# Attention's result and the normalised residual of six tiles: transposed by DMA as 16-bit planes

## The chip, the cores and the metric

The kernel runs on one core of a Trainium2 chip. The metric is the time on the device in microseconds (us). TensorE is called PE in the profile (its weight loads PEld), VectorE DVE, ScalarE ACT, GpSimd POOL and SyncE SP. The kernel before takes 514.92 us, the median of three runs (514.51 to 515.2).

## The reference

One transformer block on 2,048 positions of 512 features, in float32: layer norm, attention with 32 heads of 16 features, in which each position sees itself and seven others at distances 2, 4, ... 14, the product with `wo`, the residual; then layer norm, a product with `w1` (1,792 features), relu squared, a product with `w2`, the residual.

```python
def _A_ref(x, wqkv, wo):
    qkv = (x @ wqkv) ...                       # 32 heads of 16
    off = jnp.arange(8) * 2
    idx = pos[:, None] - off[None, :]          # masked where below zero
    logits = jnp.einsum("bhsd,bhswd->bhsw", q, kg) * scale
    o = jnp.einsum("bhsw,bhswd->bhsd", _softmax(logits), vg)
    return o.reshape(B, S, D) @ wo
def _B_ref(x, w1, b1, w2, b2):
    h = jnp.einsum("bsd,df->bsf", x, w1) + b1
    r = jnp.where(h > 0, h, 0)
    return jnp.einsum("bsf,fd->bsd", r * r, w2) + b2
h = x + _A_ref(_layernorm(x), wqkv, wo)
out = h + _B_ref(_layernorm(h), w1, b1, w2, b2)
```

## The kernel before

**Tiles.** The positions are cut into 16 tiles of 128 rows (t = 0 to 15), four of which make a unit u. Every product is made in three: each float32 operand is split into a high part in the format of the fast matmul (`hi`, L140, a cast on ACT) and a low part, the rest (`lo`, L143, a subtraction). `mm3` (L216) multiplies high by high, low by high and high by low, 4 matmuls each over the four blocks of 128 features.

**Transposes.** A product needs its left operand with features on the partitions. `transposes` (L196) turns the four 128x128 blocks of a tile by four matmuls with an identity into a PSUM bank. `o_T` (L562) turns attention's result o of a tile and has ACT take the high part (`hi_T`) and DVE the low part (`lo_T`) from the bank. `h_T` (L610) does so with the normalised residual `hn`, into the tiles `hh` and `hl` that the product with `w1` reads. For the last unit (tiles 12 to 15) `last_h_T` (L632) and `split_last` (L645) also form sums and differences of blocks, for a scheme with fewer products.

**Order of the work.** It is written out by hand; each engine runs its instructions in the order of the program. The program is cut into slots. `at(d, ...)` puts a chore into the list of the slot d later, `after` into a second list. `end_slot` (L112) issues the first list, then as much of attention as fits (`pump`, L409), then the second list. Attention (`attention`, L267) is a stream of steps on DVE with a cost for each; `pump` takes steps until DVE's planned time reaches PE's, the costs being multiplied by `SLOW` (1.01 in the first phase, then 1.12, then 1.08). POOL adds up the weighted values (`add_up`, L398). `pump(until=s)` first issues what is left of attention for tiles 2s and 2s+1.

**Phases.** First the product with `wqkv`, its results stored to DRAM in chains from which attention loads windows of keys and values. In the later part of this phase (`first_phase`, L918) tiles 0 to 3 go through attention's tail, `wo` and the norm. Then the loop at L997 makes three passes u = 0, 1, 2, each of 17 slots. In slot p, PE runs `mlp1` (L790: the product with `w1` for one block of 128 hidden features, 12 matmuls; p < 14) and `mlp2` (L797: that with `w2` for the block three slots earlier, 12 matmuls; p > 2). Beside them run the next unit's tiles t = 4(u+1) + i: `load_h` (slots LH), `o_T` (slots OP = 6, 7, 12, 13), `wo_product` (L596, slots WP = 8, 9, 13, 14; it stands ahead of `mlp1` in its slot), and `h_T` in slots 15 and 16 (14 and 15 in pass 2). After that comes a last stage for tiles 12 to 15.

`wo_product` issues its 12 matmuls and orders four chores: `h_add` (L575; DVE adds the residual and takes the statistics with `norm_stats`, L148: a statistics and an aggregate instruction; POOL then makes the reciprocal root), `h_norm` (L581; ACT applies the norm into `hn`), `add_b2` (POOL) and `spill` (to DRAM). `act_stats` (L169) is another way to the statistics, used for some tiles of x: ACT sums the row, then the squares of the differences from the mean.

**What is shared.** In the loop `mm0` and `mm1` are the only PSUM banks for `mlp1`, `wo` and the transposes, taken in turn; ACT's relu (`hidden`, L781) frees that of `mlp1` in the next slot. Rows of 128 x 512 come from one pool of 15 buffers (`row`, L96). All loads and stores but a few go through SP's queue, in order: windows (L243, L256), weights (L959), stashed low parts of `w2` (L989, L994), x (L560), the residual (L590, L594). A DMA that must wait holds those behind it.

Of the kernel before, what the change touches and what calls it, by code (L numbers as in the profile page):

```python
# [7 lines left out]

F32 = mybir.dt.float32
F32R = mybir.dt.float32r  # L10
AF = mybir.ActivationFunctionType
ALU = mybir.AluOpType
X = mybir.AxisListType.X
# [2 lines left out]
P = 128  # L16
KB = D // P
FB = F // P
R = 4
RI = 2  # L20
# [7 lines left out]
NEG = -4.0e9  # L28
ROWS = 15
LAG = 3  # L30
SLOW = 1.01, 1.12, 1.08
DELAY = 3
WJ = 2
XT = (9, 11), (7, 8)
OT = 4, 5, 10, 12
WO = 7, 9, 13, 15
HT = 20, 20, 21, 23
W2 = (18,)
LH = 3, 4, 10, 11
OP = 6, 7, 12, 13  # L40
WP = 8, 9, 13, 14
HP = 15, 15, 16, 16
UP = 14, 14, 15, 15
HL = (14, 0), (14, 1), (15, 0), (15, 1)
# [8 lines left out]
def block_kernel(ctx, tc, x, wqkv, wo, w1, b1, w2, b2, out):  # L53
# [159 lines left out]
            lo(nc.vector, d, src, h)  # L213
            dve(0.16 + 0.53 / len(h_dst))

    def mm3(ps, lh, ll, rh, rl, mid=None, at_=2 * KB):  # L216


        terms = [(lh, rh, k) for k in range(KB)] + [(ll, rh, k) for k in range(KB)]
        terms += [(lh, rl, k) for k in range(KB)]  # L220
        for n, (l, r, k) in enumerate(terms):
            if mid and n == at_:
                mid()
            nc.tensor.matmul(ps, l(k), r(k), start=(n == 0), stop=(n == 3 * KB - 1))  # L224
# [337 lines left out]
    def o_T(t):  # L562
# [9 lines left out]
        at(0, hi_T, tr, [oT[t][0]])  # L572
        at(0, lo_T, tr, [oT[t][0]], [oT[t][1]])

    def h_add(t, ps):  # L575
        h = hs[t]
        nc.vector.tensor_tensor(out=h, in0=ps, in1=h, op=ALU.add)
        dve(0.7)
        norm_stats(t, h)

    def h_norm(t):  # L581
        hn[t] = row("hn")
# [13 lines left out]
    def wo_product(t, slots):  # L596
        ps = turn["mm"].tile("wo")
        oh, ol = oT.pop(t)
        mm3(ps, lambda k: oh[:, k, :], lambda k: ol[:, k, :],
            lambda k: wo_h[:, k, :], lambda k: wo_l[:, k, :])  # L600
        for n, (fn, a) in zip(slots, ((h_add, (t, ps)), (h_norm, (t,)), (add_b2, (t,)),
                                      (spill, (t,)))):
            (after if fn in (h_norm, spill) else at)(n + (fn is add_b2), fn, *a)
# [314 lines left out]
    def first_phase(t0):  # L918
        def chores(m):
            if t0 + 3 < 16:  # L920
                if m in (0, 2):
                    at(0, x_stats, t0 + 2 + m // 2)

                early = t0 == 12
                if m + early in (6, 7):
                    at(0, x_norm, t0 - 4 + m + early)
                if m in XT[early]:
                    x_T(t0 + 2 + XT[early].index(m))
            if t0 + 5 < 16 and m in (6, 9):
                at(0, load_x, t0 + 2 + m // 3)  # L930
            if jobs and m % 3 == 0:
                at(0, weight_job)
            k = t0 // 2 * 12 - 72 + m
            if k == 19:
                dve(HOLD)
            for t in range(R):
                if k == OT[t]:
                    at(0, load_h, t)
                    o_T(t)
                if k == WO[t]:  # L940
                    wo_product(t, (1, 3, 4, 6))
                    now["pe"] += 2.73
                if k == HT[t]:
                    h_T(t)
            if k in W2:
                at(0, load_w2, W2.index(k))

# [49 lines left out]
    for u in range(R - 1):  # L997
# [11 lines left out]
        for i in js:  # L1009
            t = R * (u + 1) + i  # L1010
            if not end:
                a = i // 2 if u == 2 else 0
                for p, *what in ((LH[i] - a, at, 0, load_h, t), (OP[i] - a, o_T, t),
                                 (WP[i] - a, wo_product, t, (0, 1, 2 + 3 * a, 3 + 3 * a))):
                    todo.setdefault(p, []).append(what)
                p, h = (HP[i], i % 2) if u < 2 else HL[i]
                (todo, halves)[h].setdefault(p, []).append((h_T, t))
            todo.setdefault(UP[i], []).append((at, 0, unspill, R * u + i))
        if u == 2:
            for p, *what in ((12, at, 0, t_load, 0), (12, at, 0, t_load, 1), (13, after, 0, t_sums, 0),  # L1020
# [122 lines left out]
```

## Time and profile before

| | |
|---|---|
| time, median of 3 runs | 514.92 us (514.51 to 515.2) |
| span of the profiled execution | 513.0 us; no other time of that execution is shown |
| PE busy | 506.4 us, 2,508 matmuls |
| PEld busy | 429.3 us |
| DVE busy | 376.7 us |
| POOL busy | 350.0 us |
| ACT busy | 256.2 us |
| the loop at L997 | 165 to 436 us of the span |
| transposes of o and of hn on PE (L199, L638) | 64 and 64, 0.27 us each, overlapping |
| granted PE clock | full throughout |

The profile is one execution. Matmuls overlap in their records, so that four transposes of 0.27 us take less than four times that in the chain of work; the chain, which follows the last instruction back to what released each step, gives their share of the time. A wait of an engine is put down to the last thing that released it.

### The profile page before, as it was taken

To read this page: it belongs to the slowest core of one execution; us is meant where nothing else is said; L and a number is where in the kernel's file an instruction comes from. 1 tells how busy PE (TensorE), PEld (TensorE's weight loads), DVE (VectorE), ACT (ScalarE), POOL (GpSimd) and SP (SyncE) were. 2 spreads that over 40 slices of the span, in tenths; PEclk is the share of its full clock that TensorE was granted. 3 is DMA by queue.
4 is the path that set the end of the run, shared out by engine and by line. 5 is a ranking of instruction groups with operands and counts; after the bars stand their busy time and mean duration, and the time that the engine had idled before them with its cause. 6 is when DMAs were issued, how large, how long until landed. Compare 5 with 4: busy or idle time off the path is not lost.

```text
span 513.0 us, 7625 instructions
## 1 busy us (share of the span) xinstructions
PE 506.4 (99%) x2508; PEld 429.3 (84%) x2508; DVE 376.7 (73%) x524; ACT 256.2 (50%) x498; POOL 350.0 (68%) x430
## 2 busy tenths in 40 slices
PE   7999999999999999999999999999999999999997
PEld 6999788888888888888888888888888888989996
DVE  5489799988998798976889799778984035742333
ACT  4634687767424763463364334336432525666542
POOL 4714888894885895896778759676889544685520
PEclk9999999999999999999999999999999999999999
DMA  9677989889677895685487537557632352454112
GB/s 265 193 221 188 271 283 315 275 274 278 196 234 201 291 299 173 175 232 180 129 266 229 163 94 231 174 160 257 219 94 65 106 159 84 142 145 145 63 41 82
DMA packets 88239, 97.37 MB, mean 190 GB/s; under 512 B 8328, under 2 KB 56712, under 8 KB 88200
## 3 DMA queue, kind: packets, MB, share of 16 engines
q1 hardware_dynamic: 87256, 96.37, 61.4%
q10 hardware_dynamic: 944, 0.52, 0.3%
q8 instruction: 19, 0.31, 0.3%
q14 instruction: 20, 0.16, 0.1%
HBM read 72.65 MB, written 24.25 MB: 189 GB/s over the span
## 4 chain that ended last, share of the span: by engine, by line
PE 92%; POOL 3%; DMA 2%; DVE 1%; issue 1%; ACT 1%; SPq 0%; POOLq 0%; ACTq 0%
PE mm L224 45%; PE acc L808 29%; PE wo L224 9%; PE mm L731 6%; PE tr L199 4%; DMA wraw<-in_A_wqkv_dram 1%; DMA qkv_d<-y 1%; POOL pr L403 1%; POOL h L587 1%; POOL tl L144 0%; PE half L831 0%; SPq L432 0%; POOL wo_l L144 0%; DVE pr L346 0%; DVE ex L369 0%
## 5 line engine op out<-in xcount | busy, mean ns | idle before, releaser
L403 POOL TENSOR_TENSOR pr<-pr 128x512 f32<-128x512 f32 (+1 forms) x128 | 132.1, 1032 | 51.2 <-DVE pr L346 45.7
L224 PE MATMUL mm<-big_l,w_h 128*128 128x512 f32 x336 | 89.5, 392 | 0.0
L346 DVE TENSOR_TENSOR pr<-ex,v 128x1024 f32<-128x1024 f32 x64 | 78.0, 1221 | 11.6 <-POOL o L403 7.6
L335 DVE TENSOR_TENSOR pr<-qp,k 128x1024 f32<-128x1024 f32 x64 | 76.8, 1201 | 5.7 <-ACT qp L264 5.7
L369 DVE TENSOR_REDUCE ex<-pr 128x64 f32<-128x1024 f32 x64 | 78.4, 1225 | 1.8
L224 PEld LDWEIGHTS mm<-big_l,w_h 128*128 128x128 f32 x336 | 62.3, 188 | 12.8 <-DVE ol L144 0.2
L144 POOL TENSOR_TENSOR rl<-r,rh 128x512 fp32r<-128x512 f32 x42 | 55.4, 1318 | 22.5 <-ACT rh L141 22.4
L224 PE MATMUL mm<-big_h,xl 128*128 128x512 f32 (+1 forms) x208 | 55.9, 379 | 0.2 <-DVE xl L144 0.2
L224 PE MATMUL mm<-big_h,xh 128*128 128x512 f32 (+1 forms) x208 | 53.5, 378 | 0.7 <-ACT xh L141 0.7
L784 ACT ACTIVATE r<-mm,b_sb 128x512 f32<-128x512 f32 x42 | 28.8, 686 | 47.9 <-PE mm L224 46.1
L224 PE MATMUL mm<-big_l,xh 128*128 128x512 f32 (+1 forms) x208 | 52.7, 375 | 0.0
L808 PE MATMUL acc<-big_l,rh 128*128 128x512 f32 x190 | 52.7, 391 | 0.0
L808 PE MATMUL acc<-big_h,rh 128*128 128x512 f32 x190 | 52.3, 392 | 0.0
L808 PE MATMUL acc<-big_h,rl 128*128 128x512 f32 x190 | 51.8, 390 | 0.0
L493 ACT COPY y<-mm 128x512 f32<-128x512 f32 (+1 forms) x52 | 28.6, 552 | 40.0 <-PE mm L224 30.1
L224 PE MATMUL mm<-big_l,w_l 128*128 128x512 f32 x168 | 45.0, 390 | 0.0
L224 PEld LDWEIGHTS mm<-big_h,xh 128*128 128x128 f32 x208 | 37.6, 188 | 7.0 <-ACT xh L141 1.7
L224 PEld LDWEIGHTS mm<-big_l,xh 128*128 128x128 f32 x208 | 38.2, 188 | 6.0
L224 PEld LDWEIGHTS mm<-big_h,xl 128*128 128x128 f32 x208 | 37.2, 188 | 5.7 <-DVE xl L144 0.6
L808 PEld LDWEIGHTS acc<-big_h,rl 128*128 128x128 f32 x190 | 35.7, 188 | 7.5
L808 PEld LDWEIGHTS acc<-big_l,rh 128*128 128x128 f32 x190 | 35.4, 188 | 7.3
L808 PEld LDWEIGHTS acc<-big_h,rh 128*128 128x128 f32 x190 | 34.8, 188 | 6.5
(148 smaller groups left out, 879.8 us busy)
## 6 DMA issues: line engine op xcount, KB each, us to landing
k<-qkv_d SPq DMA_DIRECT2D x48, 288.0 KB, 2.8
v<-qkv_d SPq DMA_DIRECT2D x48, 288.0 KB, 4.0
qkv_d<-y SPq DMA_DIRECT2D x18, 512.0 KB, 4.3
big_l<-w2l_d SPq DMA_DIRECT2D x24, 256.0 KB, 3.1
xt<-in_A_x_dram SPq DMA_DIRECT2D x16, 256.0 KB, 4.3
q<-qkv_d SPq DMA_DIRECT2D x32, 128.0 KB, 3.0
h<-in_A_x_dram SPq DMA_DIRECT2D x16, 256.0 KB, 4.1
h_d<-h SPq DMA_DIRECT2D x16, 256.0 KB, 4.1
```

The lines of the kernel that those rows point to most:

```text
L144: eng.tensor_tensor(out=dst, in0=src, in1=h, op=ALU.subtract)
L199: nc.tensor.transpose(tr[:, k, :], src[:, k * P:(k + 1) * P], ident)
L224: nc.tensor.matmul(ps, l(k), r(k), start=(n == 0), stop=(n == 3 * KB - 1))
L335: nc.vector.tensor_tensor(out=pr.rearrange("p i w h d -> p i w (h d)"), in0=qps["now"][:, j % 2].unsqueeze(2).to_broadcast([P, RI, W, GC]) ...
L346: nc.vector.tensor_tensor(out=p2, in1=vwin, op=ALU.mult, in0=e1[:, :, :, j * GH:(j + 1) * GH].unsqueeze(4).to_broadcast([P, RI, W, GH, DH]))
L369: nc.vector.tensor_reduce(out=lf[:, :, :, j * GH:(j + 1) * GH], in_=pr, axis=X, op=ALU.add)
L403: nc.gpsimd.tensor_tensor(out=dst, in0=p2[:, :, :w], in1=p2[:, :, w:2 * w], op=ALU.add)
L493: nc.scalar.copy(y[:, :, t % RI * GC:(t % RI + 1) * GC], ps[:, :j * GC].rearrange("p (j c) -> p j c", j=j))
L587: nc.gpsimd.tensor_tensor(out=h, in0=h, in1=b2_sb, op=ALU.add)
L731: nc.tensor.matmul(ps, sta[y][:, k], mov[x][:, k], start=(first and q == 0), stop=(last and q == len(terms) - 1), skip_group_check=True)
L784: nc.scalar.activation(r, ps, AF.Relu, bias=b1_sb[:, f:f + 1])
L808: nc.tensor.matmul(acc[j], l[:, j * P:(j + 1) * P], w[f], start=(first and n < len(js)), stop=(last and n >= len(terms) - len(js)))
```

## The change

Six tiles are named three times, in AS, OV and HV: 4, 5, 8, 9, 12 and 13, the first two of each unit that the loop handles.

- **o (OV).** `o_T` is replaced by three chores. `o_split` (slot OP, 6 or 7) finishes the tile's attention and has ACT copy o, read as 16-bit halves, into a row `pl` of two planes, all low halves and then all high halves. `turn_dma`, at the end of the same slot, has SP issue a transposing DMA of the eight 128x128 blocks of 16-bit elements back into o's place. `o_join`, two slots later, has ACT interleave the planes again into `pl`, now transposed, then take the high part; the low part is put `after` that slot's attention.
- **wo.** `WP` moves by one slot for the first two tiles, to 9 and 10. Where the tile is in OV, `mm3` takes the products with the low part of o last (`lows_last`).
- **h (HV).** `h_T` is replaced by `h_split` and `turn_dma` in slot 12 for both tiles, `turn_join` in slot 14, and `h_parts`, which takes the high and low parts from the joined row in SBUF, in slot 15 (14 in pass 2). For tiles 12 and 13 the joined row takes the place of the PSUM bank in `split_last`.
- **Statistics (AS).** `h_add` calls `act_stats` in place of `norm_stats`.
- `SLOW` falls to 1.10 and 1.06 in the loop. `OK` and `HK` are slots for tiles of the first phase.

```diff
--- before.py
+++ after.py
@@ -8,6 +8,7 @@

 F32 = mybir.dt.float32
 F32R = mybir.dt.float32r
+U16 = mybir.dt.uint16
 AF = mybir.ActivationFunctionType
 ALU = mybir.AluOpType
 X = mybir.AxisListType.X
@@ -28,17 +29,22 @@
 NEG = -4.0e9
 ROWS = 15
 LAG = 3
-SLOW = 1.01, 1.12, 1.08
+AS = (4, 5, 8, 9, 12, 13)
+OV = (4, 5, 8, 9, 12, 13)
+HV = (4, 5, 8, 9, 12, 13)
+SLOW = 1.01, 1.10, 1.06
 DELAY = 3
 WJ = 2
 XT = (9, 11), (7, 8)
 OT = 4, 5, 10, 12
 WO = 7, 9, 13, 15
 HT = 20, 20, 21, 23
+OK = (-6, -2, 4), (-5, -1, 5), (3, 6, 10), (4, 7, 12)
+HK = (12, 15, 18), (14, 16, 19)
 W2 = (18,)
 LH = 3, 4, 10, 11
 OP = 6, 7, 12, 13
-WP = 8, 9, 13, 14
+WP = 9, 10, 13, 14
 HP = 15, 15, 16, 16
 UP = 14, 14, 15, 15
 HL = (14, 0), (14, 1), (15, 0), (15, 1)
@@ -213,11 +219,13 @@
             lo(nc.vector, d, src, h)
             dve(0.16 + 0.53 / len(h_dst))

-    def mm3(ps, lh, ll, rh, rl, mid=None, at_=2 * KB):
-
-
-        terms = [(lh, rh, k) for k in range(KB)] + [(ll, rh, k) for k in range(KB)]
-        terms += [(lh, rl, k) for k in range(KB)]
+    def mm3(ps, lh, ll, rh, rl, mid=None, at_=2 * KB, lows_last=False):
+
+
+        terms = [[(l, r, k) for k in range(KB)] for l, r in ((lh, rh), (ll, rh), (lh, rl))]
+        if lows_last:
+            terms[1:] = terms[:0:-1]
+        terms = sum(terms, [])
         for n, (l, r, k) in enumerate(terms):
             if mid and n == at_:
                 mid()
@@ -572,11 +580,65 @@
         at(0, hi_T, tr, [oT[t][0]])
         at(0, lo_T, tr, [oT[t][0]], [oT[t][1]])

+    planes = {}
+
+    def halves_of(a):
+        return a.bitcast(U16).rearrange("p (n two) -> p two n", two=2)
+
+    def two_planes(a):
+        return a.bitcast(U16).rearrange("p (two n) -> p two n", two=2)
+
+    def turn_split(key, src):
+
+        planes[key] = src, row("pl")
+        nc.scalar.copy(two_planes(planes[key][1]), halves_of(src))
+
+    def turn_dma(key):
+        src, pl = planes[key]
+        nc.sync.dma_start_transpose(
+            src.bitcast(U16).rearrange("p (n c) -> p n c", c=P), pl.bitcast(U16))
+
+    def turn_join(key):
+        src, pl = planes[key]
+        nc.scalar.copy(halves_of(pl).rearrange("p two n -> p n two"),
+                       two_planes(src).rearrange("p two n -> p n two"))
+        planes[key] = pl.rearrange("p (k c) -> p k c", k=KB)
+
+    def o_split(t):
+        s, j = divmod(t, RI)
+        pump(until=s)
+        turn_split(("o", t), o_t[s][:, j, :])
+
+    def o_join(t):
+        turn_join(("o", t))
+        tr = planes.pop(("o", t))
+        if t % R == RI:
+            ohl = att.tile([P, 2, KB, P], F32R, name="ohl", tag="o", bufs=3)
+            oT[t] = ohl[:, 0], ohl[:, 1]
+        else:
+            oT[t] = row("oh", (P, KB, P), F32R), row("ol", (P, KB, P), F32R)
+        hi_T(tr, [oT[t][0]])
+        after(0, lo_T, tr, [oT[t][0]], [oT[t][1]])
+
+    def h_split(t):
+        turn_split(("h", t), hn.pop(t))
+
+    def h_parts(t):
+        i = t % R
+        tr = planes.pop(("h", t))
+        if t // R == R - 1:
+            last_tr[i] = tr
+            split_last(i, tr)
+            return
+        hs_, ls_ = [a[:, :, i] for a in hh], [a[:, :, i] for a in hl]
+        hi_T(tr, hs_)
+        lo_T(tr, hs_, ls_)
+
     def h_add(t, ps):
         h = hs[t]
         nc.vector.tensor_tensor(out=h, in0=ps, in1=h, op=ALU.add)
         dve(0.7)
-        norm_stats(t, h)
+        (act_stats if t in AS else norm_stats)(t, h)

     def h_norm(t):
         hn[t] = row("hn")
@@ -597,7 +659,7 @@
         ps = turn["mm"].tile("wo")
         oh, ol = oT.pop(t)
         mm3(ps, lambda k: oh[:, k, :], lambda k: ol[:, k, :],
-            lambda k: wo_h[:, k, :], lambda k: wo_l[:, k, :])
+            lambda k: wo_h[:, k, :], lambda k: wo_l[:, k, :], lows_last=t in OV)
         for n, (fn, a) in zip(slots, ((h_add, (t, ps)), (h_norm, (t,)), (add_b2, (t,)),
                                       (spill, (t,)))):
             (after if fn in (h_norm, spill) else at)(n + (fn is add_b2), fn, *a)
@@ -936,12 +998,18 @@
             for t in range(R):
                 if k == OT[t]:
                     at(0, load_h, t)
-                    o_T(t)
+                    if t not in OV:
+                        o_T(t)
+                if t in OV and k in OK[t]:
+                    at(0, (o_split, lambda t: turn_dma(("o", t)), o_join)[OK[t].index(k)], t)
+                if t in HV and k in HK[t]:
+                    at(0, (h_split, lambda t: turn_dma(("h", t)),
+                           lambda t: turn_join(("h", t)))[HK[t].index(k)], t)
                 if k == WO[t]:
                     wo_product(t, (1, 3, 4, 6))
                     now["pe"] += 2.73
                 if k == HT[t]:
-                    h_T(t)
+                    (at(0, h_parts, t) if t in HV else h_T(t))
             if k in W2:
                 at(0, load_w2, W2.index(k))

@@ -1010,11 +1078,24 @@
             t = R * (u + 1) + i
             if not end:
                 a = i // 2 if u == 2 else 0
-                for p, *what in ((LH[i] - a, at, 0, load_h, t), (OP[i] - a, o_T, t),
+                o0 = OP[i] - a
+                if t in OV:
+                    turned = [(o0, at, 0, o_split, t), (o0, after, 0, turn_dma, ("o", t)),
+                              (o0 + 2, at, 0, o_join, t)]
+                else:
+                    turned = [(o0, o_T, t)]
+                if t in HV:
+                    h0 = 12
+                    turned += [(h0, at, 0, h_split, t), (h0, after, 0, turn_dma, ("h", t)),
+                               (h0 + 2, at, 0, turn_join, ("h", t))]
+                for p, *what in ((LH[i] - a, at, 0, load_h, t), *turned,
                                  (WP[i] - a, wo_product, t, (0, 1, 2 + 3 * a, 3 + 3 * a))):
                     todo.setdefault(p, []).append(what)
                 p, h = (HP[i], i % 2) if u < 2 else HL[i]
-                (todo, halves)[h].setdefault(p, []).append((h_T, t))
+                if t in HV:
+                    todo.setdefault(p, []).append((at, 0, h_parts, t))
+                else:
+                    (todo, halves)[h].setdefault(p, []).append((h_T, t))
             todo.setdefault(UP[i], []).append((at, 0, unspill, R * u + i))
         if u == 2:
             for p, *what in ((12, at, 0, t_load, 0), (12, at, 0, t_load, 1), (13, after, 0, t_sums, 0),
```

## The prediction

> **What bounds the kernel now.** I read the page's head first, then the share of the chain of work that ended last, then the busy time of each engine over the three passes of the loop at L997, which are the only place that the change touches (below).
>
> ```profile
> span 513.0 us, 7625 instructions
> PE 92%; POOL 3%; DMA 2%; DVE 1%; issue 1%; ACT 1%; SPq 0%; POOLq 0%; ACTq 0%
> 165.00:254.00 89.00, 88.98 (x409) 73.19 (x408) 73.86 (x95) 45.12 (x82) 71.14 (x77) 1.00 0.70 216
> 254.00:345.00 91.00, 91.00 (x418) 75.36 (x417) 77.65 (x98) 38.33 (x70) 66.55 (x78) 1.00 0.60 185
> 345.00:436.00 91.00, 91.00 (x420) 75.36 (x419) 54.25 (x79) 39.63 (x69) 61.97 (x71) 1.00 0.45 139
> ```
>
> The columns of the last three rows are length, then PE, PEld, DVE, ACT, POOL busy, the granted clock, the DMA share and GB/s. TensorE is busy for 270.98 of 271 us there, at full clock, and 92% of the chain is TensorE. DVE is busy for 83%, 85% and 60%, ACT for 51%, 42% and 44%. So one microsecond of TensorE work that goes is one microsecond of time, as long as TensorE doesn't then wait; any new wait of TensorE costs its full length. The span is 513.0; no other time of that execution is shown. The median of the runs is 514.92, so 1.9 us lie around the span, and I keep them. All sums are made on 513.0 and moved by 1.9.
>
> **Where the change acts.** All of AS, OV and HV are (4, 5, 8, 9, 12, 13). In the first phase only tiles 0 to 3 are handled, so OK and HK are never used, and nothing there changes. In each pass u it is tiles 4(u+1) and 4(u+1)+1, called first and second tile here. Each loses two groups of four TensorE transposes: 12 groups, 48 transposes. That is what "twelve blocks" means. Of o and hn there are 64 each now, eight of hn at L638:
>
> ```profile
> L199 PE MATMUL tr<-ident,o 128*128 128x128 f32 x64 | 9.6, 271 | 0.0
> L199 PE MATMUL tr<-ident,hn 128*128 128x128 f32 x56 | 8.3, 273 | 0.0
> L638 PE MATMUL tr<-ident,hn 128*128 128x128 f32 x8 | 1.2, 272 | 0.0
> ```
>
> **What goes from TensorE.**
>
> ```profile
> 278.64 0.44 PE tr L199 x4
> 279.08 2.77 PE mm L224 x12
> 281.85 2.72 PE acc L808 x12
> ...
> 425.83 0.44 PE tr L199 x4
> 426.27 1.39 PE acc L808 x6
> 427.66 0.44 PE tr L638 x4
> 428.10 1.40 PE acc L808 x6
> ```
>
> These are pieces of the chain in order of time: start, length, what. A group takes 0.44, and the 12 matmuls behind it 2.77 where 12 others take 2.72. So a group of o costs 0.49. Those of h split twelve matmuls into halves of 1.39 and 1.40 where half of 2.72 is 1.36: 0.44 + 0.035 = 0.475. Six of each: 6 x 0.49 + 6 x 0.475 = **5.8 us**. All of it is on the path.
>
> **What is added on ACT.** Each of the twelve blocks gets two copies of 1,024 two-byte elements per partition, and each of the six tiles gets its statistics here.
>
> ```profile
> L141 ACT CAST th<-traw 128x1024 fp32r<-128x1024 f32 x7 | 7.3, 1050 | 4.9 <-POOL traw L702 4.9
> L175 ACT ACTIVATE scrap<-xt 128x512 f32<-128x512 f32 x10 | 6.3, 633 | 0.0
> L177 ACT ACTIVATE scrap<-xt,nm 128x512 f32<-128x512 f32 x10 | 7.3, 725 | 0.3
> L176 ACT ACTIVATE nm<-nm 128x1 f32<-128x1 f32 x10 | 2.0, 203 | 0.3
> L175 ACT ACTIVATION_READ_ACCUMULATOR scrap<-xt 128x1 f32 x10 | 1.9, 192 | 0.0
> L177 ACT ACTIVATION_READ_ACCUMULATOR scrap<-xt,nm 128x1 f32 x10 | 1.9, 187 | 0.0
> L152 DVE BATCH_NORM_STATS2 st<-h 128x6 f32<-128x512 f32 x16 | 11.1, 695 | 0.5
> L153 DVE BATCH_NORM_AGGREGATE mv<-st 128x2 f32<-128x6 f32 x22 | 4.0, 182 | 0.8
> ```
>
> No two-byte copy is in the trace. The nearest row has as many elements, 1.05 us; if they went at two for one it would be about half, if the two-byte stride cost double 2.1. I take 1.05. Statistics are 0.633 + 0.192 + 0.203 + 0.725 + 0.187 = 1.94 on ACT, for 0.88 that DVE loses. So a tile adds 4 x 1.05 + 1.94 = 6.1, six of them 37 us, and ACT goes from 123 of 271 to 160, or 59%. TensorE hides that. With 2.1 it is 210, still below. The three small POOL steps behind the statistics stay three.
>
> **The transposing DMA.** No transposing DMA is in the trace either. The nearest rows are plain ones of the same 256 KB:
>
> ```profile
> h_d<-h SPq DMA_DIRECT2D x16, 256.0 KB, 4.1
> raw<-in_B_w_dram SPq DMA_DIRECT2D x14, 256.0 KB, 5.8
> out_dram<-h SPq DMA_DIRECT2D x15, 256.0 KB, 2.7
> 284.38 0.38 SPq L994 DMA_DIRECT2D big_l<-w2l_d  x1
> 290.48 2.72 PE wo L224 x12
> ```
>
> Bounds: 2.7 us to land, and eight 128x128 blocks one behind the other, 8 x 2.7 = 21.6. I take 4.1, whose source is SBUF as well. How long may it take? In pass 1 the first tile's DMA stands in SP's queue behind the windows of slot 6 and ahead of the fetch of slot 7, so it is issued at about 284.4. Its join stands in slot 8, and `wo` now in slot 9. Slot 8 starts at 290.48 less two groups (0.96), and without `wo` it lasts 5.44: TensorE wants the tile at about 295.0. Join and high part take 1.05 + 0.62, so the data must land by 293.3: a window of **8.9 us**. For the second tile the DMA is issued a slot later, about 290, and slot 9, with `wo`, lasts 8.16: about 11.5. For h there are two slots, one of them with `wo`, to the join and another to the parts. At 4.1 all is covered. While ACT waits in a join, the relu that frees a bank (L784) and the copies of q stand behind it; while SP waits for the split, the windows and fetches do; neither is long at 4.1.
>
> By the Trainium skill's page "Advanced Engine Details and Errata", X-Bar Transpose (TRN2), such DMAs are as fast as regular ones, which leaves the sum as it is. The Trainium skill's page "VectorE: DVE Perf Modes", The three transpose paths, speaks against the change: 1,309 ns for one 128x128 block by DMA, 390 on TensorE; an estimate of eight in line, 10.5 us, would be 1.6 late in each pass, 4.8 in all, and the sum 516.3. No run so far shows which.
>
> **What stays covered.** The split now waits for attention in ACT's place, where TensorE did. That has an end ahead of slot 6 (278.64):
>
> ```profile
> L403 POOL TENSOR_TENSOR o<-pr x1: 460/460/460, 274.4 to 274.4; 128x128 f32<-128x128 f32 x1
> ```
>
> **Where I expect a new wait.** The low part of o is now subtracted *behind* a whole slot of attention on DVE, and `wo` stands at the start of the next slot. `lows_last` lets eight matmuls pass first: 8 x 0.227 = 1.81 us. Is DVE behind TensorE by more than that, less the subtraction itself? DVE's waits for `wo` in the trace tell how late it is at the end of such a slot:
>
> ```profile
> 207.47 2.72 PE wo L224 x12
> 298.64 2.72 PE wo L224 x12
> 389.50 2.72 PE wo L224 x12
> ...
> 209.26 0.70 DVE L144 TENSOR_TENSOR big_l<-raw,big_h 128x512 fp32r<-128x512 f32 x1
> 301.40 0.69 DVE L577 TENSOR_TENSOR h<-wo,h 128x512 f32<-128x512 f32 x1 [0.71 <-PE wo L224]
> 392.26 0.69 DVE L577 TENSOR_TENSOR h<-wo,h 128x512 f32<-128x512 f32 x1 [1.35 <-PE wo L224]
> 293.24 0.69 DVE L577 TENSOR_TENSOR h<-wo,h 128x512 f32<-128x512 f32 x1 [1.31 <-PE wo L224]
> L144 DVE TENSOR_TENSOR big_l<-raw,big_h 128x512 fp32r<-128x512 f32 x8 | 6.9, 866 | 2.5 <-ACT big_h L141 2.5
> ```
>
> Start less idle time less the slot's start: DVE had ended the slot's attention 209.26 - 207.47 = 1.8 us after the next slot began in pass 0, 301.40 - 0.71 - 298.64 = 2.05 in pass 1, 1.4 in pass 2. That is a slot with `wo` in it, as the second tile's now is: DVE waits in it for `wo`, and its attention follows. A subtraction from SBUF takes 0.87. So the low part comes 0.85, 1.1 and 0.45 after it is wanted: **2.4 us** of TensorE waiting. The first tile's slot has no `wo`; there DVE was 293.24 - 1.31 - 290.48 = 1.45 late after waiting for a transpose in the slot before, a wait that is gone, so I count nothing; if that lateness stays, 0.5 in each pass. SLOW is lower by 0.02, which lets a little more attention into a slot; that is under 0.15 us of lateness, in the range.
>
> **The sum**: -5.8 + 2.4 = -3.4; span 509.6, time **511.5**.
>
> A last bound is the end of pass 0, where TensorE already waited for the fourth tile's normalisation:
>
> ```profile
> 252.10 0.65 PE tr L199 x4
> ```
>
> 0.65 against 0.44 is a wait of 0.2. TensorE arrives 0.95 earlier now, two groups less, and may wait up to that longer. I take nothing, since DVE's stages before it are shorter too, and keep 0.95 for the range.
>
> **The rivals.**
> Everything is covered: DVE is lighter by six times 0.88 and no longer waits for transposes, so that the low parts are in time. Time 514.9 - 5.8 = 509.1. For it: 15% of DVE is idle. Against: the lateness of 1.4 to 2.05 comes from order, not load.
> The waits eat the gain: besides 2.4, the first tiles wait 0.5 each, pass 0's end 0.95, and the join's place on ACT costs as much again, 0.2 a tile: 2.4 + 1.5 + 0.95 + 1.2 = 6.05, time 515.1, no change.
> The DMA is late, the slower side: the eight blocks go in line. Midway between the bounds, 12.2 us, the first tiles wait 12.2 - 8.9 = 3.3 each and the second 0.7: 12 us more, time 523.5. It decides from where three waits make up 3.4 us: landing at 8.9 + 1.1 = 10.0 us. For it: the moved elements are two bytes wide, which no row has. Against: the 16 engines move plain rows of this size in 2.7 to 5.8. The Trainium skill's price for a block, above, is a mild form of it.
> The change doesn't do what it says: a transposing DMA that takes SP itself for microseconds would hold the windows, and DVE with them; its signs are the third rival's.
>
> **Chances.** Forecast 0.46, covered 0.25, eaten 0.12, late DMA 0.14 and the last 0.03, both slower. Measurement can tell about 0.2%, 1 us, from no change. So faster 0.71, same 0.12, slower 0.17. The forecast's own range is 509.8 to 513.5 (its three waits from 0.25 each to 1.5). The range over the cases is **508.5 to 517.0**: below it some 0.03, above it the late DMA.
>
> **What would show it.** 80 transposes of o and hn, not 128; the passes shorter by 1.9 us each less TensorE's waits; waits of TensorE's weight loads (PEld) for the low part in the second tile's slot, on DVE, of about a microsecond; DMAs landing in under 8.9 us; ACT near 59% in the passes. If PEld waits for the high part (ACT), the DMA is the cause; if there are no waits at all, my reading of DVE's lateness is wrong. If the matmuls themselves became slower beside the DMAs, all of this is beside the point.

## The result, and the profile after

The changed kernel takes **512.18 us**, the median of 20 runs (511.36 to 514.71), the kernel before 515.0 on the same chip (20 runs, 514.16 to 519.27). The ratio is 0.9943 (95% interval 0.993 to 0.9955): 0.57%, or 2.8 us, are gone. The profiled execution took 512.31 us with a span of 510.5, so 1.8 us lie around it.

Line numbers have moved: the products are now at L232, the transposes at L205 and L700, `mlp2` at L870, high and low parts at L147 and L150, attention's DVE steps at L343, L354 and L377. The new steps are the split at L594, the transposing DMA at L598 and the join at L603.

First the head of the page of the changed kernel, its busy times, and the share of the chain.

```profile
span 510.5 us, 7598 instructions
PE 501.9 (98%) x2460; PEld 424.4 (83%) x2460; DVE 376.7 (74%) x512; ACT 290.9 (57%) x552; POOL 351.2 (69%) x430
PE 36%; DVE 4%; POOL 3%; DMA 1%; issue 1%; ACT 1%; SPq 0%; POOLq 0%; ACTq 0%
```

48 matmuls are gone from PE, 34.7 us have come to ACT. The chain's shares add up to 46% only: in this trace it is followed back no further than 274 us, and its 36% of TensorE is not to be compared with the 92% before.

The comparison that can be made is by stage, cut where the first matmul of the first product of each stage starts (so that the three passes before run from 162.80 to 435.71 us, not from 165). First the changed kernel, then the kernel before; the columns are those of the prediction's windows, and the rows are pass 0, 1, 2 and the last stage.

```profile
163.29:252.47 89.18, 89.18 (x402) 73.56 (x401) 76.77 (x95) 57.54 (x102) 73.21 (x80) 1.00 0.76 234
252.47:343.23 90.76, 89.59 (x402) 73.49 (x401) 79.25 (x95) 50.14 (x89) 69.83 (x81) 1.00 0.71 203
343.23:432.20 88.97, 88.97 (x401) 73.65 (x400) 50.50 (x67) 50.30 (x84) 59.86 (x69) 1.00 0.52 147
432.20:505.54 73.34, 73.13 (x458) 65.84 (x456) 31.59 (x59) 40.27 (x72) 36.08 (x38) 1.00 0.31 98
```

```profile
162.80:253.99 91.19, 91.17 (x418) 75.01 (x416) 76.05 (x97) 46.23 (x84) 73.05 (x80) 1.00 0.70 217
253.99:344.85 90.86, 90.86 (x418) 75.22 (x416) 77.51 (x98) 38.33 (x70) 66.55 (x78) 1.00 0.60 186
344.85:435.71 90.86, 90.86 (x417) 75.22 (x416) 54.11 (x78) 39.47 (x68) 61.97 (x71) 1.00 0.45 139
435.71:508.33 72.62, 72.48 (x458) 65.70 (x457) 30.29 (x55) 39.59 (x70) 36.09 (x38) 1.00 0.31 98
```

Here the 2.5 us between the spans come apart. Pass 0 is 2.01 shorter and pass 2 is 1.89 shorter: 16 matmuls fewer in each, and PE is busy from end to end. Pass 1 has lost the same 16 matmuls and is shorter by 0.10 only; PE stands idle for 1.17 us of it. The last stage, in which the diff takes nothing away, is 0.72 longer. The first phase, the same instructions in both, began pass 0 0.49 later in this execution, and the end after 505.54 is 0.29 longer. -2.01 - 0.10 - 1.89 + 0.72 + 0.49 + 0.29 = -2.50.

What TensorE's weight loads waited for in the passes and the last stage of the changed kernel (total, times, longest):

```profile
PEld wo L232 <- DVE ol L150: 2.0, 2, 1.0
...
PEld tr L205 <- ACT hn L200: 0.4, 1, 0.4
PEld mm L793 <- POOL tl L150: 0.3, 1, 0.3
PEld mm L793 <- DVE u L807: 0.3, 1, 0.3
PEld mm L793 <- ACT p L806: 0.2, 1, 0.2
```

The first row is the wait that the prediction named, for the low part of o. It comes twice, both times in pass 1. The second row is a transpose at the end of pass 0, which waits 0.4 for a normalised residual, as in the kernel before. The timeline of PE there (start, length, what, and in brackets the idle time before it):

```profile
295.86 1.20 PE L232 MATMUL wo<-wo_h,ol 128*128 128x512 f32 x4 [0.61 <-DVE ol L150]
...
304.88 1.21 PE L232 MATMUL wo<-wo_h,ol 128*128 128x512 f32 x4 [0.56 <-DVE ol L150]
```

And that of DVE ahead of the first, with the subtraction for the second:

```profile
291.30 1.22 DVE L354 TENSOR_TENSOR pr<-ex,v 128x1024 f32<-128x1024 f32 x1
292.56 1.23 DVE L377 TENSOR_REDUCE ex<-pr 128x64 f32<-128x1024 f32 x1
293.69 1.22 DVE L343 TENSOR_TENSOR pr<-qp,k 128x1024 f32<-128x1024 f32 x1
294.82 0.97 DVE L150 TENSOR_TENSOR ol<-pl,oh 128x512 fp32r<-128x512 f32 x1
...
304.08 0.75 DVE L150 TENSOR_TENSOR ol<-pl,oh 128x512 fp32r<-128x512 f32 x1
```

The first tile waits at 295.86, the second at 304.88. None of DVE's rows has a bracket: attention's steps stand one behind the other, and the subtraction comes when they are through. The chain of the same stretch leads elsewhere, through this dot product to the copy of `q` and its load:

```profile
288.35 4.25 DMA q<-qkv_d
```

That is a trap in reading: the load was the last thing to release the step by a semaphore, but DVE was still busy with the reduce ahead of it (292.56 + 1.23), and an earlier `q` would have moved nothing.

The pieces of the new path, as the changed kernel's instructions on the planes show them (duration in ns min/median/max, first and last start), with the landing of these DMAs in us:

```profile
L594 ACT COPY pl<-o x6: 1037/1040/1042, 187.2 to 372.5; 128x1024 uint16<-128x1024 uint16 x6
L598 SPq DMA_TRANSPOSE o<-pl x6: 1237/1270/1632, 192.9 to 380.0; - x6
L603 ACT COPY pl<-o x6: 1160/1170/1175, 198.1 to 383.8; 128x1024 uint16<-128x1024 uint16 x6
L598 SPq DMA_TRANSPOSE hn<-pl x6: 1238/1330/2922, 231.3 to 413.7; - x6
L150 DVE TENSOR_TENSOR ol<-pl,oh x6: 683/812/1017, 203.0 to 387.6; 128x512 fp32r<-128x512 f32 x6
...
DMA to landing us min/median/max: 4.3/4.7/5.1
```

And the transposes that are left on PE, by groups of lines: 40 + 36 + 4 where 64 + 56 + 8 stood.

```profile
L205 PE MATMUL tr<-ident,o 128*128 128x128 f32 x40 | 6.0, 272 | 0.0
L205 PE MATMUL tr<-ident,hn 128*128 128x128 f32 x36 | 5.3, 273 | 0.0
L700 PE MATMUL tr<-ident,hn 128*128 128x128 f32 x4 | 0.6, 272 | 0.0
```

### The profile page after: what moved, and what is told of

It reads as the page before. It is cut to its first block, busy times and chain, and to the rows that moved or that the text cites. A ratio compares the mean times of both kernels' runs of the same rounds, so it can differ in the third digit from the quotient of the medians.

```text
span 510.5 us, 7598 instructions
## 1 busy us (share of the span) xinstructions
PE 501.9 (98%) x2460; PEld 424.4 (83%) x2460; DVE 376.7 (74%) x512; ACT 290.9 (57%) x552; POOL 351.2 (69%) x430
## 5 line engine op out<-in xcount | busy, mean ns | idle before, releaser
L232 PE MATMUL mm<-big_l,w_h 128*128 128x512 f32 x336 | 88.7, 390 | 0.0
L354 DVE TENSOR_TENSOR pr<-ex,v 128x1024 f32<-128x1024 f32 x64 | 78.2, 1222 | 12.8 <-POOL o L411 6.5
L343 DVE TENSOR_TENSOR pr<-qp,k 128x1024 f32<-128x1024 f32 x64 | 76.9, 1202 | 5.6 <-ACT qp L272 5.5
L377 DVE TENSOR_REDUCE ex<-pr 128x64 f32<-128x1024 f32 x64 | 78.4, 1226 | 1.9
L232 PEld LDWEIGHTS mm<-big_l,w_h 128*128 128x128 f32 x336 | 62.8, 188 | 13.0
L150 POOL TENSOR_TENSOR rl<-r,rh 128x512 fp32r<-128x512 f32 x42 | 56.2, 1339 | 19.6 <-ACT rh L147 16.5
L232 PE MATMUL mm<-big_h,xl 128*128 128x512 f32 (+1 forms) x208 | 56.0, 379 | 0.2 <-DVE xl L150 0.2
L232 PE MATMUL mm<-big_h,xh 128*128 128x512 f32 (+1 forms) x208 | 53.5, 378 | 0.7 <-ACT xh L147 0.7
L232 PE MATMUL mm<-big_l,xh 128*128 128x512 f32 (+1 forms) x208 | 52.8, 375 | 0.0
L870 PE MATMUL acc<-big_l,rh 128*128 128x512 f32 x190 | 52.2, 390 | 0.0
L870 PE MATMUL acc<-big_h,rh 128*128 128x512 f32 x190 | 52.1, 391 | 0.0
L870 PE MATMUL acc<-big_h,rl 128*128 128x512 f32 x190 | 51.7, 389 | 0.0
L232 PE MATMUL mm<-big_l,w_l 128*128 128x512 f32 x168 | 45.0, 389 | 0.0
L232 PEld LDWEIGHTS mm<-big_h,xh 128*128 128x128 f32 x208 | 37.6, 188 | 7.0 <-ACT xh L147 1.5
L232 PEld LDWEIGHTS mm<-big_l,xh 128*128 128x128 f32 x208 | 38.2, 188 | 6.1 <-POOL big_l L150 0.2
L232 PEld LDWEIGHTS mm<-big_h,xl 128*128 128x128 f32 x208 | 37.2, 188 | 5.8 <-DVE xl L150 0.6
L870 PEld LDWEIGHTS acc<-big_h,rl 128*128 128x128 f32 x190 | 35.7, 188 | 7.5
L870 PEld LDWEIGHTS acc<-big_l,rh 128*128 128x128 f32 x190 | 35.5, 188 | 7.4
L870 PEld LDWEIGHTS acc<-big_h,rh 128*128 128x128 f32 x190 | 34.9, 188 | 6.7
```

The costliest lines, as they stand in the source:

```text
L150: eng.tensor_tensor(out=dst, in0=src, in1=h, op=ALU.subtract)
L343: nc.vector.tensor_tensor(out=pr.rearrange("p i w h d -> p i w (h d)"), in0=qps["now"][:, j % 2].unsqueeze(2).to_broadcast([P, RI, W, GC]) ...
L354: nc.vector.tensor_tensor(out=p2, in1=vwin, op=ALU.mult, in0=e1[:, :, :, j * GH:(j + 1) * GH].unsqueeze(4).to_broadcast([P, RI, W, GH, DH]))
L377: nc.vector.tensor_reduce(out=lf[:, :, :, j * GH:(j + 1) * GH], in_=pr, axis=X, op=ALU.add)
L870: nc.tensor.matmul(acc[j], l[:, j * P:(j + 1) * P], w[f], start=(first and n < len(js)), stop=(last and n >= len(terms) - len(js)))
```

## The experiments

The theory: 0.48 us go with each group of transposes, nothing of the new path is late but the low part of o, and that is late because it stands behind a slot of attention on DVE. The rivals: transposing DMAs or ACT's copies are what TensorE waits for; or the statistics and the pace of attention carry the gain, not the transposes. All kernels but the tenth are the changed kernel with the edit shown; all compute the whole reference. Their times (the median of 20 runs for the first two, of 3 to 12 for the others), with the lengths of the four stages from the trace of one execution, cut as above (us):

| kernel | median | ratio to before (95% interval) | pass 0 | pass 1 | pass 2 | last stage |
|---|---|---|---|---|---|---|
| before | 515.0 | | 91.2 | 90.9 | 90.9 | 72.6 |
| after | 512.18 | 0.9943 (0.993 to 0.9955) | 89.2 | 90.8 | 89.0 | 73.3 |
| e1_no_o | 514.31 | 0.9985 (0.9972 to 0.9997) | 89.9 | 91.4 | 89.9 | 73.3 |
| e2_no_h | 516.35 | 1.002 (1.0006 to 1.0035) | 89.9 | 93.1 | 89.9 | 72.7 |
| e3_low_first | 511.27 | 0.9925 (0.9901 to 0.9948) | 89.2 | 89.6 | 89.0 | 73.3 |
| e4_split_early | 510.73 | 0.9908 (0.9883 to 0.9933) | 89.2 | 89.6 | 88.9 | 73.3 |
| e5_dve_stats | 517.46 | 1.0037 (1.0023 to 1.005) | 90.4 | 90.6 | 91.5 | 73.4 |
| e6_slow_back | 517.2 | 1.0038 (1.002 to 1.0055) | 89.2 | 90.6 | 92.4 | 73.3 |
| e7_lows_mid | 514.6 | 0.9986 (0.9973 to 0.9998) | 89.2 | 92.6 | 89.9 | 73.3 |
| e8_dma_late | 518.68 | 1.0056 (1.004 to 1.0073) | 93.1 | 91.6 | 89.9 | 73.3 |
| e9_early_slow | 510.78 | 0.9908 (0.9895 to 0.9921) | 89.2 | 89.0 | 88.9 | 73.3 |
| e10_stats_only | 515.17 | 0.9992 (0.9978 to 1.0006) | 90.9 | 90.9 | 90.9 | 72.7 |
| e11_early_plain | 518.89 | 1.0063 (1.0039 to 1.0086) | 92.5 | 91.0 | 90.4 | 73.3 |
| e12_early_h8 | 511.76 | 0.9914 (0.9891 to 0.9938) | 89.2 | 89.6 | 89.9 | 72.7 |

The kernel before was timed again with each set: 515.0 for the first four experiments, 515.34 for e5, e7, e8 and e9, 515.15 for e6 and e10, 515.58 for e11 and e12. One of the four runs of e4 took 1023.64 us and is left out of its ratio.

**Each half alone.**

```diff
-OV = (4, 5, 8, 9, 12, 13)
+OV = ()
```

> The changed kernel with OV empty: o is transposed on TensorE again, h still by DMA, statistics still on ACT. Theory (each group taken off TensorE is worth 0.475 to 0.49 us, less what TensorE then waits for the low part of o, 1.9 us in pass 1, and 0.8 in the last stage): six groups of o come back, 2.95, and the 1.9 of waits go, so about 1 us slower than the changed kernel, 2.0 faster than the one before; no wait of TensorE at wo. Rival (the waits are made by DMAs that slow everything, h's among them): waits of a microsecond remain in the passes, and the gain over the kernel before is under 1.

```diff
-HV = (4, 5, 8, 9, 12, 13)
+HV = ()
```

> The changed kernel with HV empty: h is transposed on TensorE again, o still by DMA, statistics still on ACT. Theory: six groups of h come back, 2.85, the waits for the low part of o in pass 1 stay (1.9), the 0.8 lost in the last stage goes, since tiles 12 and 13 are in PSUM again: 2.05 slower than the changed kernel, about 1 faster than the one before. Rival (the last stage is late because everything ahead of it is shorter, not because of h's rows): the 0.8 stays, 2.85 slower than the changed kernel, no difference from the one before.

Both fell short: 0.7 us faster and 1.35 us slower than before. Passes 0 and 2 are 0.9 to 1.3 shorter, about what two groups cost; what is missing is lost in pass 1, and in the kernel without h partly in the clock: five of its twelve runs, with a mean granted clock of 0.997, took 516.61 to 517.47, the seven with 1.0 took 514.86 to 516.92. First the weight loads' waits of the kernel without o, then of the one without h:

```profile
PEld tr L205 <- ACT hn L200: 1.6, 1, 1.6
```

```profile
PEld wo L232 <- DVE ol L150: 3.4, 2, 2.3
```

Without o a transpose waits for a normalised residual; without h the low part of o is later than in the changed kernel. The price of a group stands; but the halves don't add up. The places of the waits suggest why, which was not tried further: either alone moves TensorE against DVE by another amount. The last stage tells one thing more: 72.7 without the rows of h, as before, and 73.3 in every kernel with h of tiles 12 and 13 by DMA.

**The low part ahead of attention, or a slot earlier.**

```diff
-        after(0, lo_T, tr, [oT[t][0]], [oT[t][1]])
+        at(0, lo_T, tr, [oT[t][0]], [oT[t][1]])
```

> The changed kernel with the low part of o taken ahead of the slot's attention on DVE (at in place of after in o_join). Theory (TensorE waits in pass 1 because the subtraction stands behind a slot of attention): the waits at wo go, 1.9 us, and the kernel is 4.8 faster than the one before; DVE waits for ACT's join instead, up to 3 us a tile, which its idle time takes. Rival (DVE has no slack for that; or the data itself is late): TensorE waits as much as now or longer, elsewhere, and the time is that of the changed kernel or above.

```diff
-OP = 6, 7, 12, 13
+OP = 5, 6, 12, 13
```

> The changed kernel with the split of o one slot earlier for the first two tiles (OP 5 and 6), so that the DMA, the join and the low part all come a slot earlier and wo stays. Theory: no wait for the low part, 1.9 us faster than the changed kernel, unless attention of tile 8 (which ended about 4 us ahead of slot 6) is not ready: then ACT waits some 2 us at the split in pass 1, which nothing on TensorE needs. Rival (the DMAs' own contention makes DVE late): the waits stay where they are, since DVE's attention is as late as before, and the time is that of the changed kernel.

Both take `wo`'s wait away, and pass 1 becomes 1.1 to 1.2 us shorter. In the early split, DVE writes the first tile's low part in pass 1 at 289.14, a slot ahead (first view, DVE), and TensorE comes to the third that reads it without a stop (second view, PE; no bracket):

```profile
289.14 0.68 DVE L150 TENSOR_TENSOR ol<-pl,oh 128x512 fp32r<-128x512 f32 x1
```

```profile
294.77 1.07 PE L232 MATMUL wo<-wo_h,ol 128*128 128x512 f32 x4
```

That the low part's place in DVE's order is the cause of the two waits is shown. Less came than the two waits, 2.0, because a new one stands in pass 1 of each:

```profile
PEld mm L232 <- DVE ol L150: 0.8, 1, 0.8
```

The fourth tile, whose transposes are still on PE, holds a bank until DVE has taken its low part. The early split is a better kernel than the change as it stands: 510.73, 4.3 us faster than before. The few runs do not tell it from the low part ahead of attention (511.27).

**The order inside `wo`.**

```diff
-            lambda k: wo_h[:, k, :], lambda k: wo_l[:, k, :], lows_last=t in OV)
+            lambda k: wo_h[:, k, :], lambda k: wo_l[:, k, :])
```

> The changed kernel with the three products of wo in the old order (low part of o in matmuls 5 to 8, not 9 to 12). Theory: the low part is wanted 0.91 us earlier, so both waits of pass 1 grow by 0.9 and small ones appear in passes 0 and 2: 2 us longer than the changed kernel, about 1 faster than the one before. Rival (the wait ends with something else): no change.

2.4 us longer than the changed kernel. TensorE's weight loads now wait for the low part four times:

```profile
PEld wo L232 <- DVE ol L150: 5.1, 4, 1.9
```

Four matmuls, 0.91 us, no longer stand ahead of it; the two waits grow and two more appear, 3.1 in all.

**A late DMA.**

```diff
-(o0, at, 0, o_split, t), (o0, after, 0, turn_dma, ("o", t)),
+(o0, at, 0, o_split, t), (o0 + 1, after, 0, turn_dma, ("o", t)),
```

> The changed kernel with the transposing DMA of o issued one slot later, split and join where they are. By the window of 8.9 us for the first tile, less a slot of 5.44, 3.5 us are left, and the DMA lands in 4.3 to 5.1: theory: TensorE waits for the high part of the first tile in each pass, 0.7 to 2.6 us by the changed kernel's rows, about 5.5 in all, which takes in a microsecond that it waits now: 4.5 us longer than the changed kernel, 1.5 longer than the one before; the second tile (6.1 left) waits for nothing new. Rival (what counts is DVE's lateness, and ACT's waits are hidden anyway): the time of the changed kernel.

This is the third rival's case, a late DMA: 518.68, 6.5 us over the changed kernel (5.8 by the difference of the ratios). The waits, then what followed the longest one (windows, the clock is the number ahead of the last two):

```profile
PEld wo L232 <- DVE ol L150: 3.4, 3, 2.4
PEld wo L232 <- ACT oh L147: 3.1, 2, 2.0
```

```profile
208.00:210.00 2.00, 0.36 (x2) 0.32 (x3) 2.00 (x3) 0.00 (x0) 2.00 (x2) 1.00 0.96 223
210.00:212.00 2.00, 2.00 (x6) 1.55 (x5) 1.85 (x2) 0.00 (x0) 1.84 (x3) 0.51 0.88 195
212.00:214.00 2.00, 2.00 (x7) 1.59 (x6) 2.00 (x3) 0.76 (x1) 0.40 (x1) 0.63 1.04 298
214.00:216.00 2.00, 2.00 (x11) 1.62 (x10) 1.97 (x3) 1.91 (x6) 0.42 (x1) 1.00 0.40 69
```

With the DMA a slot late the high part is waited for (ACT) in passes 1 and 2, as the prediction said it would show; in pass 0 the first tile waits for its low part instead, 2.4 us. That makes 6.5 us of waits where the changed kernel has 2.0. The 4.5 more are the number expected, but not its parts: 5.5 in all were to be for the high part, and 3.1 are. The rest is in the clock. In the profiled execution, after 2.0 us without a matmul, TensorE was granted 0.51 and then 0.63 for 4 us, 2 x 0.49 + 2 x 0.37 = 1.7 us lost. The two runs with a mean granted clock of 1.0 took 516.82 and 517.05, 4.6 and 4.9 over the changed kernel; the four with 0.993 to 0.996 took 518.41 to 519.52.

**Statistics and SLOW.**

```diff
-AS = (4, 5, 8, 9, 12, 13)
+AS = ()
```

> The changed kernel with AS empty: the statistics of the six tiles on DVE again (0.88 us each), none on ACT. Theory (DVE's lateness at the end of a slot comes from the order, since the planner fills what is left with attention): the waits at wo stay within half a microsecond of the changed kernel's, and so does the time. Rival (moving the statistics is what keeps DVE in time): the second tile's low part comes 0.88 later in each pass, and the time is 1 to 2.6 us longer.

```diff
-SLOW = 1.01, 1.10, 1.06
+SLOW = 1.01, 1.12, 1.08
```

> The changed kernel with SLOW as before (1.12 and 1.08), all else as in the changed kernel. Theory: a slot takes about 0.1 us less attention, so DVE is a little less late at the next slot, the waits of pass 1 shrink by a few tenths, but attention ends later and brings a wait at the first tile of pass 2 nearer, as with the statistics on DVE: within 1 us of the changed kernel either way. Rival (the lateness doesn't depend on the plan): no change in where TensorE waits.

Both cost about 5 us (517.46 with a before of 515.34; 517.2 with one of 515.15). I had put SLOW within 1 us and the statistics within half a microsecond, with 2.6 as the most that their rival allowed: both are misses by far. SLOW loses 3.4 us in pass 2, at the first tile's `wo`. The statistics lose 2.5 in pass 2, at the same place, and 1.2 more at the end of pass 0, where a transpose waits for a normalised residual (1.7 of this row):

```profile
PEld tr L205 <- ACT hn L200: 2.0, 2, 1.7
```

The place in pass 2 in the changed kernel (DVE, then PE):

```profile
383.20 1.23 DVE L354 TENSOR_TENSOR pr<-ex,v 128x1024 f32<-128x1024 f32 x1 [1.32 <-DMA v<-qkv_d]
384.34 0.87 DVE L150 TENSOR_TENSOR ol<-pl,oh 128x512 fp32r<-128x512 f32 x1
```

```profile
385.84 1.07 PE L232 MATMUL wo<-wo_h,ol 128*128 128x512 f32 x4
```

And with SLOW back (DVE, then PE):

```profile
383.03 1.22 DVE L354 TENSOR_TENSOR pr<-ex,v 128x1024 f32<-128x1024 f32 x1 [1.47 <-DMA v<-qkv_d]
385.88 1.23 DVE L354 TENSOR_TENSOR pr<-ex,v 128x1024 f32<-128x1024 f32 x1 [1.63 <-DMA v<-qkv_d]
387.02 1.43 DVE L150 TENSOR_TENSOR ol<-pl,oh 128x512 fp32r<-128x512 f32 x1
```

```profile
388.50 1.20 PE L232 MATMUL wo<-wo_h,ol 128*128 128x512 f32 x4 [3.13 <-DVE ol L150]
```

Here the stream of attention ends. Its last weighing steps each wait for their window of values (so does the last one in the kernel before, 1.71 us, with no transposing DMA there). With the lower SLOW the last one starts at 383.20, and the low part ends at 385.21, 0.6 us before the matmuls that read it. With SLOW back one more such step is left over, 2.85 us with its wait, and the low part, behind it in order, is 3.13 late. With the statistics back on DVE the same place shows 2.23:

```profile
389.42 1.20 PE L232 MATMUL wo<-wo_h,ol 128*128 128x512 f32 x4 [2.23 <-DVE ol L150]
```

The rest of the 5 us is again the clock. Of the twelve runs of e6, the four with a mean granted clock of 1.0 took 515.34 to 517.02, the eight with 0.993 to 0.997 took 516.44 to 519.6; of e5, the four with 1.0 took 515.98 to 516.12, the other eight 517.4 to 519.59.

**The statistics in the kernel before.** Here the edit is made to the kernel before, without anything else of the change.

```diff
-        norm_stats(t, h)
+        (act_stats if t in (4, 5, 8, 9, 12, 13) else norm_stats)(t, h)
```

> The kernel before with one part of the change alone: the statistics of tiles 4, 5, 8, 9, 12 and 13 on ACT. Putting them back on DVE made the changed kernel 5 us longer. Theory (they matter through the wait for the low part of o: with them on DVE the planner puts attention off, and DVE reaches the subtraction later): here the low part is taken before attention and TensorE doesn't wait for it, so nothing is gained: within 0.2% of the kernel before. Rival (lighter DVE is worth time by itself): 2 to 5 us faster than the kernel before.

Nothing: 0.9992 (0.9978 to 1.0006), all passes 90.9. So the statistics bring no time of their own in that kernel; they are worth 5 us in the changed one, where DVE's order has become a due time for TensorE.

**Whether the early split makes up for both.**

```diff
-OP = 6, 7, 12, 13
+OP = 5, 6, 12, 13
-SLOW = 1.01, 1.10, 1.06
+SLOW = 1.01, 1.12, 1.08
```

> e4_split_early with SLOW as before the change (1.12 and 1.08), so that each slot takes a little less attention. Theory: the wait that is left there (0.8 in pass 1, for the low part of its fourth tile on DVE, which holds a bank) shrinks or goes, since DVE is less late: 0.3 to 0.8 us faster than e4_split_early, 4.6 to 5 faster than the kernel before. Rival (attention put off comes back as a wait for the next unit's tiles): as long as e4_split_early or longer.

```diff
-AS = (4, 5, 8, 9, 12, 13)
+AS = ()
-OP = 6, 7, 12, 13
+OP = 5, 6, 12, 13
-SLOW = 1.01, 1.10, 1.06
+SLOW = 1.01, 1.12, 1.08
```

> e4_split_early with the statistics of the six tiles back on DVE (AS empty) and SLOW as before the change. Each of these two alone made the changed kernel 5 us longer. Theory (both act only through when DVE comes to the low part of o behind a slot of attention): with the low part a slot earlier neither matters, and the time is within 1 us of e4_split_early, 4 us faster than the kernel before. Rival (they are worth time by themselves): 3 us or more longer than e4_split_early.

With the split early SLOW is worth nothing (510.78 against 510.73): that its 5 us hang on the low part of o is shown. The 0.3 to 0.8 us expected on top do not show in the times, though the wait of 0.8 is gone and pass 1 is 0.6 shorter. For the statistics the same theory fell: 518.89, 8 us more (516.41 to 517.73 in the four runs with a clock of 1.0, 517.96 to 521.93 in the eight with 0.99 to 0.997). The longest waits of e11 in the passes, and the one for a low part of o:

```profile
PEld tr L205 <- ACT hn L200: 3.4, 1, 3.4
PEld tr L205 <- POOL o L411: 2.0, 1, 2.0
...
PEld mm L232 <- ACT r L846: 1.3, 1, 1.3
...
PEld mm L232 <- DVE ol L150: 0.4, 1, 0.4
```

No `wo` waits for the low part of o; the 0.4 is a product's, for a bank, as in the early split. A transpose waits 3.4 for a normalised residual, at the end of pass 0 where e5 had lost time too, another for attention itself, a product for a bank. With the statistics and the old SLOW the lateness comes out at several places, not only at the low part. SLOW alone does not bring it (e9); whether the statistics alone do, or only both, stays open: the early split with the new SLOW and the statistics on DVE was not run.

**The rows of h in the last stage.**

```diff
-HV = (4, 5, 8, 9, 12, 13)
+HV = (4, 5, 8, 9)
-OP = 6, 7, 12, 13
+OP = 5, 6, 12, 13
```

> e4_split_early with h of tiles 12 and 13 transposed on TensorE again (HV 4, 5, 8, 9). Theory (the 0.7 that the last stage loses comes from the rows in SBUF that take the place of PSUM banks there): the last stage takes 72.7 us from its first to its last product, as in the kernel before, not 73.3, and pass 2 gains 0.95 less: 0.3 us longer than e4_split_early. Rival (TensorE reaches the last stage earlier than its data, whatever the rows): the last stage still loses 0.7 or more, and the time is 0.95 longer.

The last stage is 72.7 again, 0.65 less; pass 2, which has its two groups back, is 0.95 longer. So tiles 12 and 13 by DMA gain 0.95 and give back 0.65. The times, 511.76 and 510.73 from two sets with overlapping ratios, are too near each other to add to that.

## Why the prediction was right, and where not

**The 5.8 us of transposes: right.** Passes 0 and 2 lose 2.01 and 1.89 where 1.93 was worked out, and e1 and e2 about half each where nothing waits.

**The new path: right in its sizes.** The DMA lands in 4.3 to 5.1 us (4.1 taken, window 8.9), the copies take 1.04 and 1.17 (1.05 taken), ACT is busy for 158 us of the three passes (160). No weight load of TensorE waits for a high part; ACT itself waits 1.3 us for o's DMA, at two joins of pass 2. A late DMA would have cost, as e8 shows with 6.5 us for one slot. The rival did not come: all eight blocks of 128x128 landed within 5.1 us, like the plain rows of the same size (2.7 to 5.8), and it would have decided from a landing at 10.0. By the Trainium skill's page "VectorE: DVE Perf Modes", The three transpose paths, 1,309 ns stand for one block; the estimate of eight in line, 10.5 us, does not hold here. One sum beside it was wrong, without effect: with copies at 2.1 us ACT would be busy for 123 + 6 x (4 x 2.1 + 1.94) = 185 us, not 210.

**The wait for the low part: right in kind, near in its sum, wrong in its places.** 2.4 us were expected, 0.85, 1.1 and 0.45 at the second tiles; 2.0 came, both in pass 1. The second tile there has its 1.0 for the 1.1. The first tile, counted as nothing because DVE no longer waits for a transpose, has the other 1.0, where 0.5 was named should its lateness stay: DVE, without a gap, was late there by its load and order alone. The second tiles of passes 0 and 2 have none. That the sum still came near is luck: one place was mis-sized at nothing and two at something. The step that failed is reading DVE's lateness from the trace of before, in which it had other work in another order; what held is that a low part behind a slot of attention is late by about a microsecond where DVE is full.

**SLOW: the step was wrong.** The prediction's "that is under 0.15 us of lateness, in the range" looked at the amount of attention and not at its end. At the tail of the stream a step costs 1.22 us and a wait of up to 1.6 for its window, and one such step more or less stood ahead of the low part: 3.1 us, and with the clock 5. The forecast holds because the change carries the lower SLOW; the reason given for it not mattering is refuted by e6.

**The statistics: mis-sized.** They were priced as 0.88 us a tile off DVE, and hidden. They bring nothing by themselves (e10) and 5 us in the changed kernel (e5), at the low part of o in pass 2 and at the end of pass 0.

**The last stage: missed.** 0.7 us were lost there, which no term of the sum held. e2 and e12 put them on the rows of h of tiles 12 and 13. How these delay it is not shown: the waits of the first product (0.3 + 0.3 + 0.2, after the sums and differences of its blocks) stand where only the first was before.

**The rivals.** All covered, 509.1: the early split comes to 510.73, so most of this was to be had, by a slot and not by the change as it stands. The end of pass 0, kept with 0.95, waited no longer than before; with the statistics back on DVE it did (e5), so that this bound was a real one. The span is 510.5 for 509.6: the three passes are 4.0 shorter where 3.4 was expected, the last stage 0.7 longer, and 0.8 is in the first phase and at the end, in this one execution, where nothing was changed.

## What to carry to other kernels

Work taken off the engine that bounds is all gained only where what replaces it has no new due time: look at which instruction of another engine it now waits for, and what stands ahead of that one in the same order. Ask above all what stands there at the end of a stream, where each step waits for its load; a planner's factor that is worth nothing in the middle can decide there. Where the new path has slack in front, as here between the end of attention and the product, start it a slot earlier: that was worth half as much again as the change itself (4.3 us for 2.8), and with it the factor stopped mattering. It did not make the change safe against everything: with the old factor and the statistics back on DVE as well, the early split was slower than the kernel before.

## What the runs showed of the hardware

**A short stop of TensorE can cost more than its length.** After 2.0 us without a matmul in e8 the clock fell to 0.51 and 0.63 for 4 us. It is not certain: in the profiled execution of e6 the clock stayed at 1.00 behind a stop of 3.13 us, while eight other runs of that kernel had 0.993 to 0.997 in the mean. Where TensorE's longest stop in the passes is 1.9 to 3.1 us (e2, e5, e6, e8, e11), 33 of 54 runs had a mean clock of 0.997 or less; in e7, where it is 1.5, none of 11; in the changed kernel, where it is 0.6, three of 20, which took 514.12 to 514.71. Such stops are not the only way to it: the kernel before, whose passes have none (TensorE is busy for 272.89 of 272.91 us), shows it in 8 of the 85 runs beside the experiments. By the Trainium skill's page "TensorE: Matmul & The Clock Gate", Part 1, the clock halves after an idle window of about 3.4 us that runs free of the kernel; that it depends on the moment agrees with these runs, but here 2.0 us of waiting were enough.

**A transposing DMA holds SP longer than a plain one.** Nine of the twelve issues take 1.24 to 1.36 us of SP, the longest 2.92. A plain load of values in the same kernel:

```profile
L251 SPq DMA_DIRECT2D v<-qkv_d x56: 319/320/633, 23.4 to 379.7; - x56
```

The twelve take 17.6 us of SP, 14 more than twelve plain loads, in a queue that has windows of attention behind them. No wait of TensorE leads to that in the trace; whether attention's loads were issued later for it was not tried. From issue to landing the windows take no longer than before (medians 2.8 us for k, as before, and 3.2 for v, 4.0 before); the loads of q do (4.7 for 3.0).
